# Rows of tokens that no expert gets: given a place behind the buckets instead of an index out of bounds

## The chip, the core and the metric

The kernel runs on one core of one Trainium2 chip. Its time is the device time of one execution in microseconds (us), the median over the runs shown. The engines are PE (TensorE: matmuls and weight loads), DVE (VectorE), ACT (ScalarE), POOL (GpSimd) and SP (SyncE, which only issues transfers here). Each takes its instructions in the program's order, and they wait for each other by semaphores.

## What is computed

The reference is a long convolution by FFT, whose result is the input of a mixture of experts. Cut to what matters:

```python
B, S, D, E, F = 4, 11456, 128, 8, 1024
u = x * v
y = irfft(rfft(u, 2 * S) * rfft(h_filt, 2 * S))[:, :S]     # along the sequence
x = (x * y).reshape(B * S, D)                              # 45824 tokens of 128 numbers

do_compute = x @ w_skip > 0          # the others leave as they came
xc = x[do_compute]
logits = xc @ w_gate                 # 8 experts
e_idx = argmax(logits, axis=1)
gate_w = softmax(logits)[range, e_idx]
for e in range(E):
    mask = e_idx == e
    y[mask] = gate_w[mask] * (relu(xc[mask] @ w1[e]) @ w2[e])
out[do_compute] = xc + y
```

A token whose score `x @ w_skip` isn't above 0 goes to no expert: its output is its input.

## The kernel before, in words

It has four stages. `first_phase` and `freq_phase` do the convolution by transforms that are written as matmuls, and leave its spectrum in HBM (`zd`). `out_phase` turns it back, makes the tokens and routes them. `late_slots` runs the experts over most of the tokens.

**The out phase** goes over 32 chunks (`NCH`) of 128 x 12 tokens (128 partitions, `NT` = 12 tokens in each; 45,824 tokens and padding, 49,152 rows in all). A chunk has three blocks of four tokens a partition. For each block SP loads `zt` (480 KB of `zd`) and `ox` (256 KB of the input) five blocks ahead; `product` makes `y` on PE (L862) and multiplies it by `ox` on DVE into the tile `xm` (L863), which has five buffers; `turn`, `score` and `score2` transpose it (L875, copied out on ACT at L877), take the scores (L883, ACT L885) and turn them back (L889). SP stores each block's tokens to `out` (L867). Once per chunk `choose` and `count` find each token's expert, its rank among the tokens of that expert so far, the gate's value and the token's own row number, which go to columns D and D + 1 of `xm` (L922, L923).

**`route`** then works out where each token's row of `xm` (W = 130 numbers, 520 bytes) goes in the HBM tensor `xs`. `xs` has a bucket of CAP rows for each of the eight experts. `me` is 8 for the first expert down to 1 for the last and 0 for a token that no expert gets. `rs` is the rank less CAP times `me` (L935), and `to = rs + E * CAP` (L937). A token without an expert has rank 0 here, so its `to` is E * CAP. That is one above the bound given to the transfer, and such a row isn't written. POOL issues twelve indirect transfers per chunk (L939, reached through `row_write`), each of 128 rows, one per partition, with its index from one column of `to`.

**Around it**, a hand-written list of steps sets the order: in each step one block's product, the later parts of earlier blocks, and pieces of `work`, which runs 31 early slots of 256 tokens through their expert (matmuls at L604 to L606 and L670, ACT at L632). Four times the ranks so far are turned into a table of such slots (`table`). SP reads a slot's rows from `xs` (L548) after the scatters of the chunks that the table covers have landed. The last table, after the last chunk, gives the late slots.

**The semaphores**: an indirect transfer adds to one of eight (DMASW0 to 7, in turn), and POOL doesn't issue the next on the same one before the last has landed. The first product of a chunk (L863) writes a buffer of `xm` that was scattered five chunks before, so it waits on those eight, on transfers of SP's queue and on PE; the other two products of a chunk wait only on one load and on PE.

**The late phase** runs 62 slots (PE without a gap), and POOL scatters their results to `out` by row number (L610: two transfers of 128 rows per slot, and two more for each early slot, whose results were held in HBM). There a row of `xs` that holds no token has the number 2^20, which is out of bounds too.

Of the kernel before, what the change touches and what calls it, by code (L numbers as in the profile page):

```python
# [10 lines left out]
F32 = mybir.dt.float32  # L11
# [4 lines left out]
ALU = mybir.AluOpType  # L16
# [3 lines left out]
B, S, D = 4, 11456, 128  # L20
E, F = 8, 1024
NB = 3
K1, N2 = 60, 64
L = K1 * N2
H2 = N2 // 2
# [3 lines left out]
W = D + 2  # L29
T = 256  # L30
CAP = 46080
DUMMY = E * CAP
OOB = 1 << 20

EARLY = ((3, 4), (5, 5), (8, 8), (13, 14))
# [16 lines left out]
def tables():  # L52
# [43 lines left out]
    shift[:, 1] = e[:, None] <= e[None, :]  # L96
    bump = np.where(e < E - 1, CAP, 2 * DUMMY)
    f = np.float32
# [335 lines left out]
class Experts:  # L434


    def __init__(self, tc, i, out, xs, held, mc, wf):
# [28 lines left out]
        nc.vector.memset(self.fill[:, :, D + 1:], float(OOB))  # L466
        nc.sync.dma_start(xs[DUMMY:DUMMY + T].rearrange("(j p) w -> p j w", p=128), self.fill)

# [6 lines left out]
    def table(self, cnt, tab, last, base, limit, pool, ps):  # L475
# [31 lines left out]
        nc.vector.scalar_tensor_tensor(row[:, 0:limit], self.iota[0:1, 0:limit], float(T), r, ALU.mult, ALU.add)  # L507
        nc.vector.tensor_scalar(tab[:, base:base + limit, 0], row[:, 0:limit], float(DUMMY), None, ALU.min)
        nc.vector.tensor_scalar(row[:, 0:limit], e, float(E - 1), float(F), ALU.min, ALU.mult)
# [34 lines left out]
    def load(self, tb, pool, since=None):  # L544
        nc = self.nc
        off = nc.sync.value_load(tb[:, 0:1], min_val=0, max_val=DUMMY)
        xt = pool.tile([128, 2, W], F32, name="xt", bufs=6)
# [253 lines left out]
def out_phase(tc, i, out, zd, xs, ex, consts):  # L801


    nc = tc.nc
    NT = NS
    NCH = H2
    with (
# [3 lines left out]
      with (  # L811
# [114 lines left out]
        def route(ch):  # L926
            xm, oh, top, me = chunks.pop(ch)
            nc.tensor.matmul(rk, tri, oh, start=True, stop=False)
            nc.tensor.matmul(rk, ones, top[:, 0:NT], start=False, stop=True)
            sel = ob.tile([128, NT, E], F32, name="sel")  # L930
            nc.vector.tensor_tensor(sel, rk, oh, ALU.mult)
            nc.vector.tensor_copy(scan[0][:, PAD], top[:, NT])
            rs = ob.tile([128, NT], F32, name="rs")
            nc.vector.tensor_reduce(rs, sel, axis=AX.X, op=ALU.add)
            nc.vector.scalar_tensor_tensor(rs, me, float(-CAP), rs, ALU.mult, ALU.add)  # L935
            to = ob.tile([128, NT], I32, name="to", bufs=3)
            nc.vector.tensor_scalar(to, rs, float(E * CAP), None, ALU.add)  # L937
            for t in range(NT):
                ex.row_write(nc.gpsimd.indirect_dma_start(  # L939
                    out=xs, out_offset=bass.IndirectOffsetOnAxis(ap=to[:, t:t + 1], axis=0),  # L940
                    in_=xm[:, t, :], in_offset=None, bounds_check=E * CAP - 1, oob_is_err=False), f"rows{ch}")
            cnt = None
            if ch in checks or ch == NCH - 1:
                cnt = ob.tile([128, E], F32, name="cnt")
                nc.vector.tensor_copy(cnt, top[:, NT])
            return cnt
# [19 lines left out]
        def routed(ch):  # L966
            cnt = route(ch)
            if ch in checks:
                tables.append(table(ch, cnt, ex.early, False, *checks[ch]))
            if ch == NCH - 1:  # L970
                tables.append(table(ch, cnt, ex.late, True, 0, NTAB))
# [41 lines left out]
def program(tc, i, out):  # L1013
    nc = tc.nc
    x1d = [nc.dram_tensor(f"x1d{h}", (K1, 2, N2, (NS + NB) * DH), F32).ap() for h in range(2)]
    zd = nc.dram_tensor("zd", (H2, 2, K1, 2, 2, NS * DH), F32).ap()
    xs = nc.dram_tensor("xs", (DUMMY + T, W), F32).ap()
    held = nc.dram_tensor("held", (NEARLY, 128, 2, W), F32).ap()
# [57 lines left out]
```

## Time and profile before

| | us |
|---|---|
| median of 3 runs | 2079.26 (2076.66 to 2084.81) |
| the profiled execution | 2061.02 |
| its span, first to last instruction | 2059.3 |
| convolution, up to | about 827 |
| scatters of the out phase, first to last | 877 to 1636 |
| late slots, from | about 1640 |

| engine | busy us | share of the span |
|---|---|---|
| PE | 1695.4 | 82% |
| DVE | 1207.1 | 59% |
| POOL | 1090.9 | 53% |
| ACT | 890.2 | 43% |

Times in the rows are from one profiled execution. A row of a wait names what ended it: "remote" means that the semaphore moved and no instruction of the trace was found that moved it then, and "issue" that the engine waited for nothing that the profile shows. A wait for several semaphores is put down to the one that came last by the profile. Ends of matmuls are modelled, starts are recorded. PEclk is TensorE's granted clock, in tenths on the page and as a share elsewhere.

### The profile page before, as it was taken

The page shows a single profiled execution, that of the slowest core. Times are in us where ns is not written, and L with a number is a line of the kernel's source. Part 1 is how long each engine was busy: PE and PEld are TensorE (multiplying, and loading weights), DVE is VectorE, ACT ScalarE, POOL GpSimd, SP SyncE. Part 2 cuts the span into 40 slices and gives each one's busy share as a digit, 9 for nine tenths or more (in the row PEclk, how much of TensorE's full clock was granted, in tenths as well). Part 3 has the DMA queues.
Part 4 walks back from the last instruction along what each step waited for, and adds up shares of the span by engine and source line. Part 5 has one row for each costly group of instructions (what it writes and reads, how often), then busy time and mean ns, then how long its engine had stood idle before and what let it go on. Part 6 is the DMA issues. An engine that isn't in the chain of part 4 may idle for free. (4 is left out here: it accounts for less than half of the span.)

```text
span 2059.3 us, 29369 instructions
## 1 busy us (share of the span) xinstructions
PE 1695.4 (82%) x9450; PEld 1199.3 (58%) x9450; DVE 1207.1 (59%) x2070; ACT 890.2 (43%) x1512; POOL 1090.9 (53%) x816
## 2 busy tenths in 40 slices
PE   4978799999999999633877766666785699999997
PEld 2545455555566655211555544444454599999997
DVE  2434397877899999223333333333332278998996
ACT  3645344545444443111333222223233367777775
POOL 0000186676799999155454544444545426566565
PEclk9989899999999999776888787777888799999999
DMA  9999899999889985986566565554652122222221
GB/s 238 348 272 327 277 265 320 319 314 328 243 232 292 291 256 157 203 222 162 151 167 159 153 158 136 137 152 133 183 148 78 47 70 65 68 65 61 66 64 48
DMA packets 303002, 379.80 MB, mean 184 GB/s; under 512 B 24524, under 2 KB 238916, under 8 KB 302527
## 3 DMA queue, kind: packets, MB, share of 16 engines
q1 hardware_dynamic: 220600, 291.42, 49.8%
q10 hardware_dynamic: 64007, 62.57, 9.9%
q0 software_dynamic: 18240, 23.92, 3.9%
q8 instruction: 76, 1.25, 0.3%
q14 instruction: 79, 0.65, 0.1%
HBM read 216.88 MB, written 174.99 MB: 190 GB/s over the span
## 5 line engine op out<-in xcount | busy, mean ns | idle before, releaser
L939 POOL DMA_INDIRECT xs<-xm,to x384 | 381.4, 993 | 425.2 <-DVE to L937 192.0
L399 PE MATMUL zps<-y,c 128*128 128x512 f32 x720 | 339.4, 595 | 0.0
L368 POOL TENSOR_TENSOR y<-y,p 128x1024 f32<-128x1024 f32 x120 | 282.9, 2357 | 88.7 <-DVE y L366 84.0
L863 DVE TENSOR_TENSOR xm<-y,ox 128x512 f32<-128x512 f32 x96 | 66.3, 690 | 344.1 <-PE y L862 127.3
L366 DVE TENSOR_TENSOR p<-xp,g 128x1024 f32<-128x1024 f32 x180 | 218.2, 1212 | 44.7 <-PE xp L372 29.2
L610 POOL DMA_INDIRECT out<-o,ids x124 | 168.8, 1361 | 140.0 <-DVE o L617 118.6
L366 DVE TENSOR_TENSOR y<-xp,gc 128x1024 f32<-128x1024 f32 x180 | 218.3, 1213 | 21.4 <-PE xp L372 21.4
L582 DVE TENSOR_TENSOR ws<-wf,ws 128x1024 fp32r<-128x1024 f32 x155 | 189.2, 1221 | 44.7 <-issue 36.8
L372 PEld LDWEIGHTS xp<-x,c 128*128 128x128 f32 x720 | 137.2, 191 | 99.2 <-issue 76.5
L399 PEld LDWEIGHTS zps<-y,c 128*128 128x128 f32 x720 | 134.7, 191 | 99.4 <-issue 89.6
L372 PE MATMUL xp<-x,c 128*128 128x256 f32 x720 | 186.5, 382 | 4.2 <-DVE p L366 4.2
L355 POOL TENSOR_TENSOR g<-gc 128x256 f32<-128x256 f32 x60 | 50.7, 845 | 261.4 <-ACT gc L353 261.4
L400 ACT COPY z<-zps 128x512 f32<-128x512 f32 x180 | 103.9, 586 | 191.1 <-PE zps L399 189.5
L577 ACT CAST ws<-wf 128x1024 fp32r x155 | 161.6, 1043 | 17.3 <-issue 12.9
L670 PEld LDWEIGHTS bank<-wd,h 128*128 128x128 f32 x992 | 134.1, 215 | 54.1 <-issue 53.9
L353 ACT COPY gc<-t 64x384 f32<-64x384 f32 x240 | 113.5, 473 | 119.6 <-DVE y L366 68.1
L670 PE MATMUL bank<-wd,h 128*128 128x128 f32 x992 | 146.8, 304 | 13.4 <-issue 12.9
L885 ACT COPY lt<-bank 128x128 f32<-128x128 f32 x96 | 25.5, 266 | 294.6 <-remote 127.1
L862 PE MATMUL y<-zt,c 120*64 120x512 f32 x384 | 132.6, 751 | 24.4 <-DMA ox<-xo 12.4
L724 DVE SCALAR_TENSOR_TENSOR hh<-hp,hh 128x1024 fp32r<-128x1024 f32 x124 | 150.9, 1217 | 1.5 <-ACT hh L723 1.5
L604 PE MATMUL hp<-hl,ws 128*128 128x256 f32 x496 | 150.3, 303 | 1.6 <-DVE hh L724 0.7
L159 ACT COPY wf<-ps 120x512 f32<-120x512 f32 x192 | 110.5, 589 | 92.9 <-PE ps L158 47.4
(149 smaller groups left out, 3696.5 us busy)
## 6 DMA issues: line engine op xcount, KB each, us to landing
x<-x1d SPq DMA_DIRECT2D x60, 960.0 KB
x1d<-wf ACTq DMA_DIRECT2D x48, 960.0 KB
zd<-z SPq DMA_DIRECT2D x120, 384.0 KB
zt<-zd SPq DMA_DIRECT2D x96, 480.0 KB
out<-xm SPq DMA_DIRECT2D x96, 260.0 KB
ox<-xo SPq DMA_DIRECT2D x96, 256.0 KB
wf<-x SPq DMA_DIRECT2D x48, 480.0 KB
wf<-v SPq DMA_DIRECT2D x48, 480.0 KB
```

The costliest lines, as they stand in the source:

```text
L366: nc.vector.tensor_tensor(o, x[:, None].broadcast_to([128, 2, B, D]), v[:, :, None, :].broadcast_to([128, 2, B, D]), ALU.mult)
L368: add = lambda o, v: nc.gpsimd.tensor_tensor(o, o, v, ALU.add)
L372: nc.tensor.matmul(x[:, :, k], c2[:, k], x1[:, k, blk * B:(blk + 1) * B, :], start=True, stop=True)
L399: nc.tensor.matmul(zps, c3[:, a, :], y[:, blk, a], start=(a == 0), stop=(a == 1))
L577: nc.scalar.copy(w[:, 0], (self.w1f, self.w2f)[which][:, ds(self.where(nc.scalar, tb), F)])
L582: eng.tensor_tensor(w[:, 1], src[:, ds(self.where(eng, tb), F)], w[:, 0].bitcast(F32), ALU.subtract)
L604: nc.tensor.matmul(hp, w[:, 0, c], hl[:, 0], start=True, stop=False)
L610: ins = nc.gpsimd.indirect_dma_start(out=self.rows, out_offset=bass.IndirectOffsetOnAxis(ap=ids[:, j:j + 1], axis=0), in_=o, in_offset=Non ...
L670: nc.tensor.matmul(bank[:, j * D:(j + 1) * D], h[f // 2][:, f % 2, j * 128:(j + 1) * 128], wd[s][:, f * D:(f + 1) * D], start=(f == 0), st ...
L724: nc.vector.scalar_tensor_tensor(h[:, 1], hp, 0.0, h[:, 0].bitcast(F32), ALU.max, ALU.subtract)
L862: nc.tensor.matmul(y[p * 64:(p + 1) * 64], c4s[ch // C4][:, ch % C4, p, :], z[:, 2 * p:2 * p + 2], start=True, stop=True)
L939: ex.row_write(nc.gpsimd.indirect_dma_start(out=xs, out_offset=bass.IndirectOffsetOnAxis(ap=to[:, t:t + 1], axis=0), in_=xm[:, t, :], in_o ...
```

## The change

Two constants move: `xs` gets 49,152 rows (32 x 128 x 12) behind the eight buckets, from REST = E * CAP on, and the dummy slot moves behind them. In `route` one instruction of DVE becomes two. The first makes `tz`, which is the token's own row number where `rs` is 0 or above, which is where no expert gets it, and 0 elsewhere. The second makes `to = rs + REST + tz`. The bound of the scatter is now the end of the new rows, so every index lies inside and every row is written. Nothing reads the new rows.

```diff
 CAP = 46080
-DUMMY = E * CAP
+REST = E * CAP
+DUMMY = REST + H2 * 128 * NB * B
@@ route
             to = ob.tile([128, NT], I32, name="to", bufs=3)
-            nc.vector.tensor_scalar(to, rs, float(E * CAP), None, ALU.add)
+            tz = ob.tile([128, NT], F32, name="tz")
+            nc.vector.scalar_tensor_tensor(tz, rs, 0.0, xm[:, :, D + 1], ALU.is_ge, ALU.mult)
+            nc.vector.scalar_tensor_tensor(to, rs, float(REST), tz, ALU.add, ALU.add)
             for t in range(NT):
                 ex.row_write(nc.gpsimd.indirect_dma_start(
                     out=xs, out_offset=bass.IndirectOffsetOnAxis(ap=to[:, t:t + 1], axis=0),
-                    in_=xm[:, t, :], in_offset=None, bounds_check=E * CAP - 1, oob_is_err=False), f"rows{ch}")
+                    in_=xm[:, t, :], in_offset=None, bounds_check=DUMMY - 1, oob_is_err=False), f"rows{ch}")
```

On DVE, between two products of an early chunk of the out phase, there stands before:

```order
L863 TENSOR_TENSOR xm<-y,ox 128x2x4x64 [waits DMAHW7_49,PE_49]
L931 TENSOR_TENSOR sel<-bank_4813,scan_4807 128x96 [waits PE_49]
L932 COPY scan_4807<-top 128x8
L934 TENSOR_REDUCE rs<-sel 128x12 [waits DVE_49]
L935 SCALAR_TENSOR_TENSOR rs<-me,rs 128x12 [waits DVE_49]
L937 TENSOR_SCALAR to<-rs 128x12 [waits DVE_49]
L495 COPY tcum<-bank_4814 8x1 [waits Activation_49]
```

And at the same place after it (lines from L863 on count one or three more):

```order
L864 TENSOR_TENSOR xm<-y,ox 128x2x4x64 [waits DMAHW7_49,PE_49]
L932 TENSOR_TENSOR sel<-bank_4813,scan_4807 128x96 [waits PE_49]
L933 COPY scan_4807<-top 128x8
L935 TENSOR_REDUCE rs<-sel 128x12 [waits DVE_49]
L936 SCALAR_TENSOR_TENSOR rs<-me,rs 128x12 [waits DVE_49]
L939 SCALAR_TENSOR_TENSOR tz<-rs,xm 128x12 [waits DVE_49]
L940 SCALAR_TENSOR_TENSOR to<-rs,tz 128x12 [waits DVE_49]
L496 COPY tcum<-bank_4814 8x1 [waits Activation_49]
```

One row is added in each of the 32 chunks, with a wait on DVE's own result and on no other engine; POOL, PE, ACT and SP issue the same instructions in the same order as before.

The first product of a chunk stands on DVE like this, before and after alike (here before):

```order
L903 SCALAR_TENSOR_TENSOR me<-bank_4813,mw 128x12 [waits DVE_49]
L906 TENSOR_TENSOR scan_4807<-rev,me 128x96 [waits DVE_49]
L863 TENSOR_TENSOR xm<-y,ox 128x2x4x64 [waits DMASW5_49,DMASW4_49,DMASW6_49,DMASW3_49,DMASW7_49,DMASW2_49,DMAHW0_49,DMASW1_49,DMAHW5_49,DMASW0_49,PE_49]
L918 TENSOR_TENSOR scan_4808<-scan_4807 128x104 [waits DVE_49]
L918 TENSOR_TENSOR scan_4809<-scan_4808 128x104 [waits DVE_49]
```

Nothing moves there. The waits on transfers (DMASW, DMAHW) are instructions of their own ahead of the product, and PE's is carried by the product itself.

## Rows read from the trace of the kernel before

**Rows 1.** The page's 40 slices: busy tenths of PE and of DMA.

```profile
PE   4978799999999999633877766666785699999997
DMA  9999899999889985986566565554652122222221
```

**Rows 2.** Busy time by stage: columns named in the first line.

```profile
core 0: us, PE busy (x) PEld busy (x) DVE busy (x) ACT busy (x) POOL busy (x), PEclk, DMA share, GB/s
259.00:827.00 568.00, 567.80 (x1799) 332.03 (x1798) 499.68 (x437) 260.57 (x492) 465.63 (x235) 1.00 0.90 274
877.00:1640.00 763.00, 500.20 (x3277) 333.36 (x3270) 247.56 (x924) 212.87 (x412) 381.36 (x384) 0.78 0.54 147
1640.00:2051.00 411.00, 403.76 (x3370) 401.25 (x3369) 354.38 (x578) 286.60 (x386) 228.35 (x185) 1.00 0.23 64
```

**Rows 3.** Waits from 877 to 1640 us: us in total, times, longest.

```profile
POOL xs L939 <- DVE to L937: 192.0, 20, 14.1
ACT lt L885 <- remote: 127.1, 17, 23.7
...
DVE xm L863 <- remote: 108.0, 12, 22.6
DVE xm L863 <- PE y L862: 102.9, 29, 14.2
...
ACT h L632 <- remote: 63.5, 19, 7.7
```

**Rows 4.** Line L863 on DVE: durations min/median/max in ns, and idle before it.

```profile
L863 DVEq EVENT_SEMAPHORE  x228: 21/50/50, 845.7 to 1576.8; - x114
...
  remote: 108.0, 12
  DMA xs<-xm,to: 40.5, 6
```

**Rows 5.** Instructions in order, PE and DVE, one chunk (start, us, idle before).

```profile
1206.25 1.08 PE L862 MATMUL y<-zt,c 120*64 120x512 f32 x4
...
1217.27 0.69 DVE L863 TENSOR_TENSOR xm<-y,ox 128x512 f32<-128x512 f32 x1 [9.81 <-remote]
...
1226.08 1.08 PE L862 MATMUL y<-zt,c 120*64 120x512 f32 x4
...
1227.20 0.69 DVE L863 TENSOR_TENSOR xm<-y,ox 128x512 f32<-128x512 f32 x1
```

**Rows 6.** POOL in the same stretch: first and last scatter of a chunk.

```profile
1200.65 0.97 POOL L939 DMA_INDIRECT xs<-xm,to  x1 [7.97 <-DVE to L937]
...
1214.83 0.97 POOL L939 DMA_INDIRECT xs<-xm,to  x1 [0.30 <-issue]
1227.42 0.97 POOL L939 DMA_INDIRECT xs<-xm,to  x1 [11.62 <-DVE to L937]
```

**Rows 7.** Lines L939 and L610 on POOL: durations min/median/max in ns.

```profile
L939 POOL DMA_INDIRECT xs<-xm,to x384: 966/972/1955, 877.1 to 1635.5; - x192
L610 POOL DMA_INDIRECT out<-o,ids x124: 969/972/1824, 1677.3 to 2052.0; - x124
```

**Rows 8.** DMA queues from 877 to 1640 us: packets, MB, share of 16 engines.

```profile
q1 hardware_dynamic: 81589, 99.26, 48.3%
q0 software_dynamic: 12288, 12.02, 5.7%
```

**Rows 9.** The queue of POOL's transfers from 1640 us on.

```profile
q0 software_dynamic: 5952, 11.90, 8.8%
```

**Rows 10.** Waits from 1640 us on that PE ended.

```profile
ACT yt L739 <- PE my L734: 93.2, 61, 2.4
DVE o L617 <- PE mto L704: 5.3, 3, 3.1
```

**Rows 11.** Small instructions on DVE from 1000 to 1640 us: busy, mean ns.

```profile
L937 DVE TENSOR_SCALAR to<-rs 128x12 int32<-128x12 f32 x26 | 4.5, 173 | 1.3 <-DVE rs L935 0.5
L935 DVE SCALAR_TENSOR_TENSOR rs<-me,rs 128x12 f32<-128x12 f32 x26 | 4.4, 171 | 0.9
```

## The prediction

> **What bounds the kernel now.** I read the slices first, then busy time by stage, then the waits of the one stage that the change touches.
>
> The slices [rows 1] show PE nearly always busy in most of the convolution and in the late slots, and with gaps between them, in the out phase. Busy time by stage [rows 2] says the same in numbers. In the convolution and in the late slots PE is busy without a gap (567.8 of 568 us, 403.8 of 411 us). Between 877 and 1640 us no engine is: PE 500 of 763 us at a granted clock of 0.78 (against 1.00 in the two others), POOL 381, DVE 248, ACT 213, and DMA has a share of 0.54. So this stage is held by waits, and what the change is worth is read from them.
>
> The largest are DVE's in front of the product (L863) and ACT's in front of what it copies out of PSUM (L885, L632), many ended by "remote", by nobody that the trace can name [rows 3]. The list for L863 [rows 4] adds 40.5 us put down to the scatter, "DMA xs<-xm,to". That would be the plain story: DVE waits until an old buffer of `xm` has been scattered. One row speaks against it. The waits on transfers stand on DVE as instructions of their own ahead of the product, and the longest of all 228 took 50 ns. What is left is the wait that the product carries itself, on PE. So PE's signal is what comes late.
>
> The instructions in order show it [rows 5]. PE starts the four matmuls of one product at 1206.25 and needs 1.08 us; DVE takes the result at 1217.27, ten microseconds after their modelled end. Twenty microseconds on, the same four matmuls start at 1226.08 and DVE takes their result at 1227.20, 0.04 us after the end. POOL tells the two apart [rows 6]: the first falls into a run of twelve scatters (1200.65 to 1215.80, the last start plus 0.97), and DVE starts 1.5 us after the run; the second comes just ahead of the next run. So PE's signals come late while scatters run.
>
> In the late slots POOL scatters too, about as densely (186 in 411 us against 384 in 763), and there the longest wait on PE that this theory would touch is 2.4 us in 61 and 3.1 us in 3 [rows 10], with no "remote" among them. Two things differ. The late scatters come in twos and threes, not in twelves. And their rows are nearly all written: the queue moved 11.90 MB for 186 x 128 rows, 500 bytes a row [rows 9], while in the out phase it moved 12.02 MB for 384 x 128 rows, 245 bytes of 520 [rows 8]. So 47% of the rows of `xm` are written there, about 23,100, and 26,000 are dropped. The change takes away just these.
>
> **The change part by part.**
>
> *One instruction of DVE more per chunk.* Its like takes 171 to 173 ns [rows 11]; 32 x 0.173 = 5.5 us. DVE is busy 248 of 763 us, so most of it lies beside other work; but `to` is what POOL waits for (192.0 us in 20 waits, [rows 3]), so I count all 5.5. Behind `tz` on DVE stand the next products; its wait is on DVE itself, and ends with the instruction before.
>
> *POOL.* A scatter takes 972 ns in the median with half its rows dropped and 972 with nearly all written [rows 7]. So making the indices valid costs POOL nothing: 0, from equal rows.
>
> *DMA.* 26,000 rows of 520 bytes are 13.5 MB more in a stage that moves 112. In engine time: from 1640 us the queue takes 8.8% of 16 engines for 419 us, 590 us or 3.17 per scatter; in the out phase 5.7% for 763 us, 696 us or 1.81 per scatter. 384 x 1.36 / 16 = 33 us per DMA engine, a share of 0.58 instead of 0.54. Cover: loads are issued five blocks ahead, and their waits held DVE 50 ns at most [rows 4]. I count 0; without that cover it is up to 33 us.
>
> *The dropped rows.* No row shows a drop by itself, so this cost is bounded. At one end it is 0: the late signals belong to runs of twelve scatters, whatever their rows. At the other end every late signal goes, and POOL is what is left: 384 x (0.972 + 0.30 of idle time, [rows 6]) = 488 us for a stage of 763, 275 us less. Between them I take the waits of the product whose end the trace can't name or puts down to the scatter: 108.0 + 40.5 = 148.5 us [rows 4]. It is the nearest row, since the product is in order on DVE and everything of the next block hangs on it. ACT's waits on "remote" (127.1 + 63.5 us, [rows 3]) lie in the same stretches and are not added. Some would stay (long runs may hold signals with all rows written), some of the 102.9 us named for PE would go too; I let these cancel. What PE's clock may give back is not counted, because PE waits most of the time that it is low.
>
> **The sum**, against the profiled execution: 2061.0 - 148.5 + 5.5 = 1918 us. The median of the runs lies 18.2 us above that execution (2079.26 against 2061.02), so 1918 + 18 = **1936 us**.
>
> **The rivals.** *It changes nothing.* The change would then do what it says and gain nothing, because runs of twelve scatters hold PE's signals by themselves. For it: POOL's time per scatter is equal with and without dropped rows; the late slots have no runs of twelve, so they can't refute it. Against it: a similar density of scatters there leaves the signals alone. It gives 2079 + 5.5 = 2085 us, within 0.5% of the median (10 us, about what a measurement of this kernel can tell from no change).
>
> *It is slower by the rows.* As in the first rival, and the 33 us of DMA time aren't hidden: `zt` and `ox` come late, PE starts a product later, and the whole step moves. The price is 33 us in all, and it decides from the point where the loads need longer than five blocks. The stage's share of 0.54 says that the mean is far from it; slices of 8 and 9 just before and at the stage's start [rows 1] say that its first part is not. It gives 2079 + 5.5 + 33 = 2118 us. The Trainium skill has a rule that speaks for this rival, in "DMA: Bandwidth & Descriptors", section "Issuing engines are not separate DMA queues": transfers issued from any engine end up on the same 16 DMA engines and interleave, so rows on POOL's queue take time from SP's loads. By that rule 2118 us would be the time if the loads were late; the trace shows the shared load (0.54) but no load that held DVE.
>
> *It gains far more.* All late signals go and POOL becomes the bound at 488 us. Then 2079 - 275 + 5.5 = 1810 us. Against it: DMA at 0.58 of 763 us is 443 us of work and PE has 500 us at a mixed clock, so three engines would have to fit together almost without a gap.
>
> **How the numbers follow.** The forecast (some half to all of the product's waits, 1860 to 2030 us) has 46%, the large gain 12%, no change 22%, slower by DMA 14%. The other 6% are gains or losses of other sizes, half of them faster. Faster by over 0.5%: 46 + 12 + 3 = 61%; within: 22 + 1 = 23%; slower: 14 + 2 = 16%. The range of 1850 to 2095 us reaches over the case of no change; it leaves out most of the large gain and most of the slower case.
>
> **What would show it.** If I am right, the profile after has the stage between the first and the last scatter shorter than 763 us, PE's clock in it above 0.78, few or no waits of L863's successor, L885 and L632 on "remote", POOL's share of the stage above 0.50 with 972 ns per scatter, and 25 to 26 MB instead of 12 in POOL's queue there. If those bytes are there and the "remote" waits too, the drops were innocent, and the run of twelve is the cause. If the stage is longer and the product's waits name loads, the rows' bytes were the price.

## The result and the profile after

The changed kernel takes 2087.19 us in the median of 15 runs; the kernel before took 2077.26 us in the 15 runs beside them. The ratio is 1.0034, with an interval of 1.0018 to 1.0050: 7 us more (10 by the two medians), within the 0.5% that the prediction calls no change. The forecast was 1936 us. The rival that says "it changes nothing" gave 2085 us, and it is what happened.

The change does what it says. In the changed kernel POOL's queue moves in the out phase (877 to 1663 us) what it moved before [rows 8] and all the dropped rows beside it. Columns are packets, MB and the share of 16 engines:

```profile
q1 hardware_dynamic: 81502, 99.11, 46.5%
q0 software_dynamic: 12288, 25.58, 10.3%
```

520 bytes for each of 384 x 128 rows are 25.56 MB, so all rows are written; it is 13.56 MB more than before. Busy time by stage, to be laid beside [rows 2] (the first line names the columns; the stages are a little longer here):

```profile
core 0: us, PE busy (x) PEld busy (x) DVE busy (x) ACT busy (x) POOL busy (x), PEclk, DMA share, GB/s
259.00:827.00 568.00, 567.15 (x1795) 331.32 (x1794) 499.57 (x436) 260.48 (x492) 465.32 (x235) 1.00 0.91 274
877.00:1663.00 786.00, 500.02 (x3268) 333.77 (x3267) 252.48 (x953) 211.89 (x410) 381.32 (x384) 0.77 0.57 160
1663.00:2077.00 414.00, 406.39 (x3369) 403.93 (x3367) 354.18 (x578) 287.31 (x386) 228.96 (x185) 0.99 0.23 64
```

The out phase has the same work and the same gaps. (It is 786 us here against 763, but these are two single executions: the profiled one of before, 2061 us, is shorter than each of the 15 runs above, and this one of 2087 us is its kernel's median. The 15 runs give the change 7 to 10 us.) The waits of the out phase, beside [rows 3], in us, times and the longest:

```profile
POOL xs L942 <- DVE to L940: 195.6, 19, 13.6
DVE xm L864 <- PE y L863: 121.5, 33, 15.7
ACT lt L886 <- remote: 121.3, 18, 13.0
...
DVE xm L864 <- remote: 92.7, 15, 13.5
ACT h L633 <- remote: 88.5, 17, 9.9
```

The large waits that ended on "remote" are all still there, with no dropped row left in the stage. For the product 92.7 us of the 108.0 of before remain, and for `h` 88.5 us stand where 63.5 were. The prediction had said what this would mean: the bytes are there and the waits too, so the drops were innocent.

### The profile page after: what moved, and what is told of

It reads as the page before. It is cut to its first block, busy times and chain, and to the rows that moved or that the text cites. A ratio compares the mean times of both kernels' runs of the same rounds, so it can differ in the third digit from the quotient of the medians.

```text
span 2085.4 us, 29401 instructions
## 1 busy us (share of the span) xinstructions
PE 1696.7 (81%) x9450; PEld 1201.5 (58%) x9450; DVE 1214.3 (58%) x2102; ACT 890.8 (43%) x1512; POOL 1092.2 (52%) x816
## 5 line engine op out<-in xcount | busy, mean ns | idle before, releaser
L369 POOL TENSOR_TENSOR y<-y,p 128x1024 f32<-128x1024 f32 x120 | 283.1, 2359 | 88.5 <-DVE y L367 83.8
L864 DVE TENSOR_TENSOR xm<-y,ox 128x512 f32<-128x512 f32 x96 | 66.3, 690 | 352.5 <-PE y L863 144.0
L863 PE MATMUL y<-zt,c 120*64 120x512 f32 x384 | 130.6, 749 | 25.6 <-DMA ox<-xo 12.2
```

Of the source, the lines that this page charges most:

```text
L369: add = lambda o, v: nc.gpsimd.tensor_tensor(o, o, v, ALU.add)
L863: nc.tensor.matmul(y[p * 64:(p + 1) * 64], c4s[ch // C4][:, ch % C4, p, :], z[:, 2 * p:2 * p + 2], start=True, stop=True)
```

## The experiments

All versions compute the same outputs. Each was timed beside the kernel before on the same chip; its median there was 2078 us for the first four, 2060 for the next four, 2086 and 2062 for the last two groups, so ratios are compared, not times. Two theories stood at the start: **A**, an unbroken run of scatters holds PE's signals, whatever rows it carries; **B**, they are late by the traffic or the load of the whole stage, and the scatters only coincide with it.

**The instruction without the rows** (`tzonly`). The changed kernel drops the rows again:

```diff
-                    in_=xm[:, t, :], in_offset=None, bounds_check=DUMMY - 1, ...
+                    in_=xm[:, t, :], in_offset=None, bounds_check=REST - 1, ...
```

> The changed kernel with the bound put back to REST - 1, so that the added instruction tz stays, the index of a dropped row is a row number behind the buckets, and the row is dropped as before. If the 7 us that the change cost (2087 against about 2079) are the instruction on the path to POOL (32 x 0.17 = 5.5 us by the prediction), this runs at 2084 to 2087 us too. If they are the 13.5 MB more that are written, it runs at 2079 to 2081 us. If dropped rows had a price that written rows merely replaced by another, the two would differ by that.

Its queue moved what it moved before the change (877 to 1655 us):

```profile
q0 software_dynamic: 12288, 12.02, 5.6%
```

It took 2086.18 us, 1.0032 times the kernel before (0.9999 to 1.0065), which is the changed kernel's ratio. So the 7 us fit the instruction and leave nothing for the rows; the interval, some 14 us wide, would hide a few us either way.

**Breaks in the run** (`gap3`, `gap6`, `gap1`). The kernel before, with an addition of POOL on a spare tile ahead of some of the twelve scatters:

```diff
+GAPS = (3, 6, 9)        # gap6: (6,); gap1: 1 to 11, with 64 columns
+PAUSE = 512
@@ route
+        def pause():
+            nc.gpsimd.tensor_tensor(spare, spare, spare, ALU.add)
...
             for t in range(NT):
+                if t in GAPS:
+                    pause()
                 ex.row_write(nc.gpsimd.indirect_dma_start(
```

> The kernel before with a pause of POOL (an addition on a spare 128x512 tile; between the 0.85 us of a 128x256 and the 2.36 us of a 128x1024 in the trace, so an estimated 1.35 us) ahead of the 4th, 7th and 10th scatter of each chunk. Theory A, an unbroken run of scatters holds PE's signals and they get out 1.5 us after it: the signals get out in each pause, they are late by 4 us at most where it was up to 20, the chain to the next 'to' moves while POOL scatters, and the stage comes to 650 to 720 us: 1970 to 2040 us in all. Theory B, the signals are late by the traffic of the whole stage or by something that only meets the scatters in time: nothing moves or the waits stay, and the stage grows by the pauses that aren't hidden: 2079 to 2210 us (3 x 1.35 x 32 = 130 us if every pause is on the path).

> The same with one pause only, ahead of the 7th scatter. Theory A: the signals get out once in the middle of a run, so part of the gain of the three pauses: 2010 to 2065 us. Theory B: 2079 to 2122 us (1.35 x 32 = 43 us).

> The same with a short pause (64 columns in place of 512, an estimated 0.4 us) ahead of each scatter but the first, about the same added time as three pauses, spread evenly. If signals need a pause that is longer than some part of a microsecond to get out, they stay late as in a run of twelve, and the longer run (12 x 1.27 + 11 x 0.4 = 20 us) makes it slower: 2100 to 2220 us. If only the rate of scatters counts (theory A in another form: POOL's rows come faster than they drain), this gains as much as three pauses or more: 1950 to 2040 us.

Three breaks took 1893.88 us, 0.911 of the kernel before (0.906 to 0.916), though POOL has 103 us more to do. One break took 0.9615 (0.957 to 0.966), eleven short ones 0.926 (0.922 to 0.931). The gain was larger than theory A had put it in each of the three. This is POOL in the version with three breaks, beside [rows 6]: start, duration, the idle time before and what ended it.

```profile
1179.93 0.97 POOL L949 DMA_INDIRECT xs<-xm,to  x1 [0.30 <-issue]
1181.21 0.97 POOL L949 DMA_INDIRECT xs<-xm,to  x1 [0.30 <-issue]
1182.20 1.06 POOL L932 TENSOR_TENSOR spare<-spare 128x512 f32<-128x512 f32 x1
1183.42 0.99 POOL L949 DMA_INDIRECT xs<-xm,to  x1 [0.17 <-issue]
...
1198.72 0.97 POOL L949 DMA_INDIRECT xs<-xm,to  x1 [1.47 <-DVE to L945]
```

At 1198.72 a new chunk begins, 1.47 us after the last one's end; before it was 8 to 12 us [rows 6], and POOL's wait for `to` falls from 192.0 us in all [rows 3] to 47.5. That is where the time came from: the chain that leads to the next `to` runs while POOL scatters. The waits in this version's out phase (872 to 1487 us):

```profile
ACT lt L887 <- remote: 60.3, 12, 11.8
...
POOL xs L949 <- DVE to L945: 47.5, 8, 30.5
...
DVE xm L865 <- PE y L864: 44.0, 22, 8.1
...
ACT h L634 <- remote: 26.2, 11, 3.8
DVE xm L865 <- remote: 17.9, 4, 5.7
```

and its busy time, columns as in the stages above:

```profile
872.00:1487.00 615.00, 479.26 (x3379) 326.14 (x3380) 297.25 (x949) 214.56 (x422) 490.94 (x480) 0.86 0.70 186
```

The product's wait on "remote" falls from 108.0 us [rows 3] to 17.9, with one break it is 54.9. ACT's wait for `lt` falls less, from 127.1 us to 60.3: three breaks let many of the signals out in time, not all. The stage takes 615 us in place of 763, PE's clock in it rises from 0.78 to 0.86, and POOL is busy for 491 us, with some 100 us of gaps between its instructions (288 of 0.30 and 96 of 0.17 us): now it is nearly the bound.

**The same additions ahead of the run** (`lead`): `GAPS = (0,)` and three additions in a row, so that the run stays whole.

> The kernel before with the same three additions of POOL per chunk as in the version with three pauses (3 x 1.07 us there), but all three ahead of the first scatter, so that the run of twelve stays whole. If it is the break in the run that gave the 184 us, this gains nothing: the additions lie in the time in which POOL waits for 'to' (some 8 us per chunk), so 2075 to 2090 us. If POOL's additions help in another way (later start of the run, another rhythm of the chunks, POOL awake), it gains a good part of it: 1890 to 2000 us.

The ratio is 0.993 (0.991 to 0.996), and the waits on "remote" stay (142.1 us for `lt`, 84.4 for the product). The additions as such bring almost nothing, and the break brings the rest. Where the 0.7% come from is open.

**How long a break must be, and how many** (`gap3s`, `gap3m`, `gap2`, `gap6x3`). Only `GAPS` and `PAUSE` change: three breaks of 64 and of 256 columns, two of 512, and one of three additions.

> Three pauses per chunk with the short addition (64 columns, 0.345 us in the even version) in place of 1.07 us. If a pause has only to end the run for a moment, signals get out as with the long ones and the stage loses 96 x 0.73 = 70 us of POOL's time, so far as POOL bounds it: 1825 to 1870 us. If what has piled up needs longer than 0.345 us to get out, the signals stay late: 1900 to 2040 us.

> Three pauses of 256 columns (an estimated 0.65 us, between 0.345 and 1.07) ahead of the 4th, 7th and 10th scatter. 0.345 us gave 0.976, 1.07 us 0.911. If what has piled up needs a certain time to get out, this lies between: 0.93 to 0.96. If 0.65 us is enough, POOL's shorter time shows: 0.89 to 0.91.

> The kernel before with two pauses of 1.07 us per chunk, ahead of the 5th and the 9th scatter. One pause gave 0.9615, three gave 0.911. If signals are late by the length of the unbroken piece, pieces of four lie between: 0.925 to 0.945. If the total of the pauses counts and POOL isn't yet the bound at two, about the same (0.93). If three pauses were already more than POOL's time allows, two are as good or better: 0.90 to 0.915.

> The kernel before with one break per chunk, ahead of the 7th scatter, of three additions in a row (3.2 us). Three breaks of 1.07 us gave 0.911, one of 1.07 us 0.9615. If the total of the pauses counts (time in which signals get out), 0.90 to 0.925. If it is the length of the unbroken pieces (six scatters), little more than the one short break: 0.945 to 0.965.

| breaks per chunk (us each, from the profiles) | total us | ratio |
|---|---|---|
| none inside, 3.2 us ahead of the run | 0 | 0.993 |
| 3 of 0.34 | 1.0 | 0.976 |
| 1 of 1.06 | 1.1 | 0.9615 |
| 3 of 0.68 | 2.0 | 0.944 |
| 2 of 1.06 | 2.1 | 0.933 |
| 1 of 3.2 | 3.2 | 0.948 |
| 3 of 1.07 | 3.2 | 0.911 |
| 11 of 0.345 | 3.8 | 0.926 |

Neither column alone orders the ratios. One break of 3.2 us is worth less than three of 1.07; three of 0.34 are worth less than one of 1.06. The 0.948 of `gap6x3` lies in the range given for the length of the unbroken pieces, not in that for the total. It looks as if something piles up during scatters and drains in breaks, but that picture is read from the table, not shown.

**The run in another place** (`late12`, `late16r`). The late slots had no late signals [rows 10], and no run of twelve. The kernel before gets six of them there, to a spare tensor that nothing reads, with 128 rows or with 16:

```diff
+            def extra():                       # ahead of the stores of every tenth slot
+                for t in range(NS):
+                    ins = nc.gpsimd.indirect_dma_start(
+                        out=self.junk[left[0] // 10], out_offset=bass.IndirectOffsetOnAxis(ap=nums[:, t:t + 1], axis=0),
+                        in_=self.fill[:, 0], ...          # late16r: nums[0:16, t:t + 1], fill[0:16, 0]
```

> The kernel before with six additional runs of twelve scatters in the late slots (every tenth slot, 128 rows of zeros each, all written to a spare tensor that nothing reads), where PE has no gap and the longest wait on it was 3 us. If an unbroken run holds PE's signals wherever it stands, ACT's and DVE's waits on PE or on 'remote' reach 5 to 20 us in these six places, PE stands still there, and the late slots take 30 to 100 us longer than 411. If it needs the out phase (its loads, its clock, its dropped rows), they stay under 3 us, and the late slots take up to some 20 us more, by POOL's results that come later (two buffers).

> The same six runs of twelve scatters, of 16 rows each in place of 128. POOL's time per scatter (0.97 us) shows whether its cost goes with the rows. If the instructions of POOL that follow each other hold the signals, the waits are as long as with 128 rows. If the rows on their way do (descriptors that the DMA engines work off), an eighth of them should leave waits under 2 us.

Waits from 1640 us on with 128 rows:

```profile
ACT yt L756 <- PE my L751: 70.9, 50, 2.2
ACT yt L756 <- remote: 44.6, 6, 17.9
...
DVE o L617 <- remote: 11.7, 4, 4.4
...
ACT hh L740 <- remote: 11.0, 5, 3.2
```

and with 16:

```profile
ACT hh L740 <- remote: 48.9, 6, 13.5
DVE o L617 <- remote: 41.8, 6, 17.4
...
ACT yt L756 <- remote: 36.8, 5, 15.7
```

There were none on "remote" in the kernel before. So a run holds PE's signals there too, in a stage where PE had a clock of 1.00 and the DMA share was 0.23 before [rows 2], and with none of the added rows dropped; and an eighth of the rows holds them as long. (The kernel's own stores queue up behind each added run, so that 19 to 27 scatters stand in a row in `late12`, not twelve. [rows 10] leaves out waits on PE of up to 6.1 us between 1640 and 1661 us; they end before the first scatter of the late phase, at 1664.1, and so can't be its doing.) A scatter of 16 rows takes POOL 0.843 us in the median, one of 128 rows 0.972 (line L716 of the two). What counts is the run of POOL's instructions, not the rows on their way. The times (2146 and 2143 us, single runs, some 85 us above the kernel before) can't carry a verdict: DVE also waited for one of the two result buffers `o`, whose scatter stands behind the run (31.4 us in 8 waits with 128 rows).

**The same runs broken** (`late12g`), and both again with six result buffers in place of two (`o6` is the control, `late12o` unbroken, `late12go` broken):

```diff
                 for t in range(NS):
+                    if t % 3 == 0:
+                        nc.gpsimd.tensor_tensor(spare, spare, spare, ALU.add)
                     ins = nc.gpsimd.indirect_dma_start(
```

> The kernel before with six additional runs of twelve scatters of 128 written rows in the late slots, which unbroken cost about 86 us, now with an addition of 1.07 us ahead of each third scatter. If breaks in POOL's row of scatters let PE's signals out there too, the longest wait on PE or 'remote' falls from 17.9 us to 6 or less, and the span lies at most 40 us above the kernel before's, though POOL has 6 x 4 x 1.07 = 26 us more to do. If POOL's time is what counts, it costs 86 to 112 us.

> The kernel before with six result buffers (o) in place of two, nothing else. It is the control of the next two; the late slots have PE without a gap and DVE's waits for these buffers are small there, so 0.995 to 1.003 by every theory.

> Six result buffers and the six additional unbroken runs of twelve scatters in the late slots. If an unbroken run holds PE's signals there too and that costs time by itself, PE stands for some 5 to 15 us in each: 30 to 90 us above the control. If the 82 us that the same runs cost with two buffers were the wait for the buffers alone, the six buffers hide the run: 0 to 15 us above it.

> The same with an addition of 1.07 us of POOL ahead of each third of the additional scatters. If breaks let the signals out, this costs less than the unbroken version although POOL has 26 us more to do: 0 to 25 us above the control. If POOL's time counts, it costs more than the unbroken one.

`late12g` took 2196 us, 110 more than the kernel before, where at most 40 were expected. Its signals did come sooner, but DVE waited longer for the two result buffers, 75.6 us where the unbroken version had 31.4 (waits from 1640 us on):

```profile
DVE o L617 <- DMA out<-o,ids: 75.6, 12, 16.0
...
ACT hh L744 <- remote: 6.7, 1, 6.7
```

6.7 us is the longest wait on "remote" there, 17.9 in the unbroken version. The control took 0.9986 (0.9968 to 1.0003), the unbroken runs with six buffers 1.042 (1.036 to 1.047), the broken ones 1.050 (1.044 to 1.055). So six buffers don't hide the unbroken runs (some 90 us above the control, where 0 to 15 were expected if the buffers were all), though no wait for a buffer is left in that trace. But by time the expectation for the breaks failed: they didn't make the runs cheap. Another reading fits the totals as well, that POOL's added time is simply paid for: 72 scatters of 0.97 us, 0.30 apart, are 92 us, and 117 with the additions, where 86 and 90 us were measured without breaks and 110 and 97 with them. These totals can't tell the two apart; the traces can say more. POOL in the broken version with six buffers, from the end of one additional run (L720) on:

```profile
1827.35 1.06 POOL L719 TENSOR_TENSOR spare<-spare 128x512 f32<-128x512 f32 x1
1828.58 2.21 POOL L720 DMA_INDIRECT junk<-fill,nums  x1 [0.17 <-issue]
1831.09 0.97 POOL L720 DMA_INDIRECT junk<-fill,nums  x1 [0.30 <-issue]
1832.37 1.24 POOL L720 DMA_INDIRECT junk<-fill,nums  x1 [0.30 <-issue]
1833.91 0.97 POOL L610 DMA_INDIRECT out<-o,ids  x1 [0.30 <-DVE hh L745]
1835.19 1.20 POOL L610 DMA_INDIRECT out<-o,ids  x1 [0.30 <-issue]
...
1850.76 0.97 POOL L610 DMA_INDIRECT out<-o,ids  x1 [0.30 <-issue]
1852.04 0.97 POOL L610 DMA_INDIRECT out<-eo,k  x1 [0.30 <-issue]
1858.17 0.97 POOL L610 DMA_INDIRECT out<-o,ids  x1 [5.16 <-DVE o L617]
```

The stores of real results (L610) had queued up behind the broken run, and POOL now makes up for them: 15 scatters from 1833.91 to 1853.01 without a break. Busy time in the two stretches, columns as above:

```profile
1810.00:1834.00 24.00, 23.79 (x199) 23.35 (x198) 24.00 (x36) 16.70 (x23) 20.56 (x17) 1.00 0.24 66
1834.00:1855.00 21.00, 7.45 (x55) 6.68 (x54) 5.67 (x10) 4.01 (x6) 14.74 (x15) 0.75 0.24 69
```

PE works without a gap beside the broken run and stands for most of the unbroken one. The last matmul of a result on PE, and ACT's copy of it out of PSUM:

```profile
1838.24 0.29 PE L755 MATMUL my<-hh,ws 128*128 128x256 f32 x1
...
1853.94 0.37 ACT L760 COPY yt<-my 128x256 f32<-128x256 f32 x1 [14.62 <-remote]
```

PE is done at 1838.53 by the modelled end, and it had gone on to start other matmuls until 1841.87; ACT hears of it at 1853.94, 0.93 us after the last scatter of the run. It is the same at the other places: every wait of ACT on "remote" of over 4 us in these late slots falls into or just behind the unbroken scatters that follow the last break, and none beside the breaks. So the breaks did let the signals out, and the additional work of POOL then made a new unbroken run of the kernel's own scatters. Part of the time is also POOL's own at the end: the last added run stands two slots before the end, and PE's last matmul ends at 2126 us (2144 without breaks), POOL's last scatter at 2147 in both. How the totals split between the two isn't shown.

**The changed kernel with breaks** (`aftergap3`): all rows written, `tz`, and three breaks of 512 columns.

> The changed kernel (every row written, instruction tz) with three pauses of 1.07 us per chunk, as in the version of the kernel before that took 0.911 of its time. If the signals were held by the unbroken run alone, and rows cost nothing, this gains the same: 0.905 to 0.918 (some 1880 to 1905 us, by the chip). If the rows that are written cost DMA time as soon as the waits no longer cover it (up to 33 us), 0.92 to 0.93. If dropped rows had a price of their own beside the run's, 0.88 to 0.90.

1897.17 us, 0.909 (0.905 to 0.912), the same as the kernel before with three breaks (0.911). Once the signals get out, the change costs nothing that can be seen: POOL is the bound, and neither the instruction on DVE nor 13.5 MB lie on its path. Its out phase:

```profile
868.00:1493.00 625.00, 487.07 (x3460) 333.99 (x3456) 317.30 (x985) 222.23 (x430) 494.56 (x480) 0.86 0.74 205
```

The DMA share is 0.74 and still hidden. Both versions with three breaks beat both kernels by 9%.

## Why the prediction was wrong, and where it was right

**What bounds the stage: right.** The prediction read that no engine binds the out phase, that DVE's wait at the product is on PE and not on transfers, and that PE's signals come late while scatters run. The breaks confirm it: nothing changed but POOL's run of scatters, and the waits on "remote" fell with the time. The trace of before says it of all 96 products, by the modelled end of the last matmul and where DVE was free: 48 ended inside a run of scatters, and DVE took 27 of them over 1 us late, by up to 21.7; 48 ended outside, and the latest was taken 1.1 us late. With all rows written it is 29 of 49 (up to 18.6 us) inside, and at most 1.0 us outside. One thing the prediction's example hides: signals don't all wait for the end of the run. Of the 27 late products 15 were taken while POOL still scattered. It shows in the run of [rows 6] too, which ends at 1215.80:

```profile
1205.30 0.43 PE L883 MATMUL bank<-xT,wg 128*32 128x128 f32 x8
...
1209.56 0.27 ACT L885 COPY lt<-bank 128x128 f32<-128x128 f32 x1 [9.66 <-PE mh L606]
...
1209.88 0.33 PE L889 MATMUL bank<-ident,lt 128*128 128x128 f32 x1 [0.92 <-ACT lt L885]
```

ACT copies out PE's scores 3.8 us after their end, in the middle of the run; the product that ended at 1207.33 was 9.9 us late. So in this run the lag grew. ACT's own signal isn't late: PE goes on 0.05 us after the copy's end (0.06 at most for all eight such copies that ended in a run while PE stood idle).

**The cause: wrong, and this is the step that failed.** In *The dropped rows* it put the cost between 0 and 275 us and took 148.5. The measured value is 0, to within the few us that the intervals leave open (the rows written and dropped, with the same instruction, give 1.0034 and 1.0032). What the term stood for, the late signals, belongs to the unbroken run of scatters: three breaks took 184 us off the time. The argument for the drops was the late slots: scatters there are as dense, and the signals are on time. But they differ from the out phase in two things at once, as the prediction itself said: their rows are written, and their scatters come in twos and threes [rows 10, 9]. Such a comparison speaks for neither. Yet the price was taken as if it spoke for the drops, and the rival, which the same text says can't be refuted by the late slots, got 22% against 46. `late12` changes one of the two alone, and the late signals appear. That 2087 us lie between 1850 and 2095 speaks for the range, which was drawn to reach over the rival, and not for the forecast.

**The terms around it: right.** The instruction `tz` takes 180 ns in the median (line L939 of the changed kernel, 32 times), 5.8 us against the 5.5 counted, and `tzonly` gives 6.6 us (0.32%) for it. POOL's scatter takes 974 ns in the median after the change, 972 before [rows 7], so 0 was right. The bytes came as worked out, the share rose from 0.54 to 0.57 (0.58 was said), and the waits on transfers ahead of the product (L864, 228 of them) still last 50 ns at most. PE, which reads `zt` itself and which the prediction left out here, waited for loads of it for 4.1 us in all before and hardly at all after. The rival "slower by the rows" falls with that. Its rule in the Trainium skill ("DMA: Bandwidth & Descriptors", section "Issuing engines are not separate DMA queues") agrees with the higher share. No run here shows time lost to loads by it: with all rows, three breaks and a share of 0.74 the waits ahead of the product still last 50 ns at most, and PE waits 6.7 us for `zt`.

**The large gain** came in part, by another key. It gave 1810 us; three breaks took 1894, about two thirds of that gain. "POOL is what is left" comes close to the version with three breaks: 615 us, of which POOL works 491.

**The rows never were the measure of a scatter's cost.** The equal 972 ns with half the rows dropped [rows 7] could have been read further: if the instruction doesn't feel its rows, what it holds up need not either. The Trainium skill says of such an instruction ("Perfetto Trace Analysis", section "DMA Instruction — SWDGE (GPSIMD)") that its recorded end is the end of making descriptors, not of moving data. The runs agree as far as they go: the instruction takes 972 and 974 ns with 12.02 and with 25.58 MB moved. 16 rows in place of 128 shorten it by 0.13 us of 0.97, and the hold not at all.

**Open** stays by what way POOL's scatters hold PE's signals and not ACT's; no run here looks inside. That rows could be written without the added instruction wasn't tried.

## What to carry to other kernels

Where engines wait for PE and the trace shows PE long done, look at what POOL does in that time: a run of a dozen indirect transfers without a break may be what holds the signal, and a microsecond of other work after every third was worth 9% here. Before a cause is priced, look for what else differs between the place that has the symptom and the place that hasn't; two differences make it no evidence. A version that delays POOL makes its later scatters come in a row, so look for the symptom there too before you judge it by time.

## What the runs showed of the hardware

- While POOL issued an unbroken run of scatters, PE's signals reached ACT and DVE late: ACT waited up to 23.7 us in the out phase (in the first run, of 24 scatters) and up to 17.9 in the late slots with 128 rows a scatter; DVE waited up to 17.4 there with 16. With every row written in the out phase the longest were 13.0 to 13.5 us, and a product was up to 18.6 us late. Outside the runs DVE took a product at most 1.1 us late.
- Part of the late signals came before the run's end (15 of 27 late products before the change); the others came within 3.9 us after it. One in the late slots came 0.93 us after it (1853.01 to 1853.94).
- ACT's signals to PE were on time in the same runs (0.06 us at most in eight cases).
- Rows that an index out of bounds drops cost neither POOL (972 ns against 974 with all written) nor the kernel anything that could be measured (1.0032 against 1.0034); neither does writing them.
- A break of POOL's own arithmetic of 1.07 us ahead of each third scatter lets most of the signals out (0.911 of the time); three of 0.34 us do less (0.976).
- A scatter of 16 rows takes POOL 0.843 us, one of 128 rows 0.972.
